# A planned attention-and-MLP kernel: two first groups of a stage interleaved, one product moved ahead in the last block, the engine order planned from longer durations

## The chip, the cores and the metric

The kernel runs on one core of one Trainium2 chip. The metric is the device time of one execution in microseconds (us), lower is better; of several runs the median counts.

## What is computed

The reference is a capped attention and two MLP blocks, each feeding the next (the weights arrive as 8-byte words, which the kernel itself turns into 4-byte floats):

```python
scores = scale * np.matmul(q, k.transpose(0, 1, 3, 2))     # 4 x 12 heads, 448 x 448, head size 64
scores = cap * np.tanh(scores / cap)
attn = np.exp(scores - max); attn = attn / (attn.sum(-1) + 1e-9)
x = (attn @ v) as 1792 tokens x 768
h = np.maximum(x @ w_in, 0.0);  x = h * h @ w_out          # 768 -> 2048 -> 768
gate = 1 / (1 + np.exp(-(x @ w_gate)));  val = x @ w_val   # 768 -> 1536
out = gate * val @ w_out2                                  # 1536 -> 768
```

## The kernel before, in words

The attention comes first and takes about the first 200 us. Then follow four **stages** (`STAGES`): two halves of 896 tokens of the first MLP (`x`, weights `w1`, `w2`), then two of the second (`y`, weights `wg`, `wv`, `wo`). Each half is worked on as a 2x2 split into blocks of 448 tokens, and the products use a Strassen scheme of seven products instead of eight. Every operand is split into a high part (fp32r, written by ACT) and a low part (written by DVE: raw minus high), so that a product of 128x128 by 128x448 is three matmuls (lines 742, 744, 745: low weight by high data, high weight by low data, high by high).

A **step** (a `unit` in the code) is one entry of TensorE's list; there are 550. `strassen` steps (nine matmuls) are named by a digit: "1" to "7", which stand for the data blocks b11 ("1"), b21 ("2"), b22 ("3") and the sums t2 ("6"), t4 ("4"), t3 ("7"), t1 ("5"). A group (two column blocks of one weight) has these seven, and within it they wait for each other: "1" and "2" meet in PSUM after an ACT copy of "1" (`pre`), "7" needs "6" copied out by ACT (`cp`), "4" needs "7" copied out, "3" needs "5" added up by DVE (`sum`). `second` steps are the products with `w2` (plain), `sums2` steps those with `wo` (again seven digits, six matmuls each, for three output columns c); a block of 21 `sums2` steps comes after each four columns (`add_block`), and works on data `gx` and `gy` that DVE and ACT make from the gated results `g`.

The list of steps is written by the loop at the end of the kernel (`add_s`, `add_q`, `add_p`, `add_block`): group after group as "12657", with "4" and "3" of the group before (`held`) behind "1" and "2" of the next. Behind TensorE, four engines run:

- DVE makes low parts, sums, the accumulations (`acc`) and four of the five operations that turn a weight into floats (lines 586, 588, 590, 592; `convert`); ACT does the first (line 230, `raw<-w`) once the attention is over, further high parts, copies out of PSUM and activations.
- POOL makes the low parts of the weights (line 733, `wl`).
- SP issues all transfers. A converted weight is written to DRAM (`s_w<-raw`) and read back (`pair<-s_w`) each time that it is used; the converter has two buffers `raw`, so the ACT operation of one weight waits for the store of the second one before it.

In which order each engine does its work isn't written by hand. A planner (`Flow`) plays the program through with a duration for each operation (`act`, `dve`, `dve1`, `dvep`, and a number at each `on(...)`) and writes each instruction down when it comes up in that play. The engines run their lists in that order, so a duration that is too short puts an instruction too early into its engine's list, and what stands behind it waits. When a weight is converted is bound to steps: `FIRST` and `AHEAD` in `convert_all` (weights of the second MLP: begin `FIRST` steps ahead of the first use, and spread from there). `early_forms` makes and stores the data blocks of the last stage as soon as its inputs are stored.

Of the kernel before, what the change touches and what calls it, by code (L numbers as in the profile page):

```python
# [14 lines left out]
ALU = mybir.AluOpType  # L15
# [14 lines left out]
SR = 32  # L30

PT, XE, TH, NV, WB = 2, 6, 2, 2, 4
WSTART, PACE, AHEAD, FIRST = 2, 2, 70, 180
# [21 lines left out]
class Flow:  # L55
# [6 lines left out]
    def __init__(self, have):  # L62
# [4 lines left out]
        self.free = {e: True for e in self.queue}  # L67
        self.pipe = 0.0
# [36 lines left out]
    def serve(self, engine):  # L105
# [11 lines left out]

        self.at(self.now + length, end)
# [27 lines left out]
    def dve(self, n):  # L146
        return lambda: (0.15 + n * 0.00104) * (1.0 if self.free["POOL"] else 1.6)

    @staticmethod
    def dve1(n):  # L150
        return 0.16 + n * 0.0005
# [13 lines left out]
def attn_mlp_kernel(ctx: ExitStack, tc: tile.TileContext, qk, v, cap, w1, w2, wg, wv, wo, out):  # L165
# [339 lines left out]
    def early_forms(src):  # L505
        w = WIDE[src[1]]
        for i in range(HK):
# [223 lines left out]
    def low(m, h, hi, lo, src, res, item):  # L731
        n = cols(src)
        yield on("POOL", 0.15 + n * 0.0023, lambda: nc.gpsimd.tensor_tensor(out=lo, in0=src, in1=f32(hi), op=ALU.subtract))  # L733
        flow.fire(("w", m, h))
        used(res, item)
# [135 lines left out]
    def sums2(u, stage, gi, num, c):  # L871
# [4 lines left out]
        elif num == "5":  # L876
            st["bank", grp, "e"] = bank(w)
# [5 lines left out]
        products(terms, o, num in "15", False)  # L883
        return shares2(grp, num, o, w)

    def shares2(grp, num, o, w):
# [15 lines left out]
        if num in "243":  # L902
            give(o)
        if num in "67" or gi < F2 // FG - 1:
            return
# [84 lines left out]
    def add_q(stage, gi, num, c):  # L990
        item = stage, "wo", gi
        if (item, num) not in spot:
# [8 lines left out]
            "3": [("out", grp, "5")]}.get(num, [])  # L1001
        units.append({"us": us(WIDE[STAGES[stage][1]], 6), "ms": [m], "needs": needs, "last": (stage, gi, num), "frees": 2, "tag": "gy" if num in "35" else "gx",
            "fn": sums2, "bank": {"1": 2, "5": 1}.get(num, 0), "args": (stage, gi, num, c)})

    def add_block(stage, gi, held, next_):
        nonlocal pairing, ahead
        order2 = [(num, c) for num in "1267453" for c in range(HK)]
        for x, (num, c) in enumerate(order2):
# [7 lines left out]
            add_q(stage, gi, num, c)  # L1016
# [18 lines left out]
    for stage, (src, _) in enumerate(STAGES):  # L1035
        kinds, kind2, ng = (("w1",), "w2", F1 // FG) if src == "x" else (("wg", "wv"), "wo", F2 // FG)
        w = WIDE[STAGES[stage][1]]
        held, wait = None, None
        for gi in range(ng):
            for j in range(2):  # L1040
                for kind in kinds:
                    grp = stage, kind, gi, j
                    for num in "12657":
                        if num != "1" or grp != ahead:
                            add_s(*grp, num)
                        if held and num in "12":
                            add_s(*held, "43"[num == "2"])
                    held = grp
                    if kind == "wg" and j == 0 and gi:
# [182 lines left out]
```

## Time and profile before

| | |
|---|---|
| time, median of 3 runs | 1165.56 us (1164.96 to 1168.18) |
| the profiled execution's own time | 1167.6 us |
| its span | 1165.8 us, mean granted TensorE clock 0.988 |
| busy: PE / PEld / DVE | 1104.3 (95%) / 924.8 (79%) / 878.9 (75%) us |
| busy: ACT / POOL | 683.1 (59%) / 491.4 (42%) us |

The page is read in this way: the busy shares tell which engine is nearest to the limit, but a busy TensorE is a modelled one; how densely its matmuls follow each other is told by counting them in a stretch. The waits tell for which engine TensorE stood still.

### The profile page before, as it was taken

Reading aid. Unit: us, or ns where it says so; the run is one execution under the profiler, and the core shown is the slowest. Engines: PE = TensorE matmul, PEld = TensorE weight load, DVE = VectorE, ACT = ScalarE, POOL = GpSimd, SP = SyncE. Lnnn points to the kernel's source line nnn. Section 1 sums busy time; section 2 is a strip of 40 time slices with the busy share of each in tenths; the row PEclk is TensorE's granted clock in tenths of the full one; section 3 lists DMA queues with packets and bytes.
Section 4 is the critical chain, followed back from the end, with each engine's and each line's share of the span. In section 5 each row is a group of like instructions: output and inputs, shape, how many; then the busy total and the mean of one; then the engine's idle time right before and its main releaser. Section 6 shows DMA issues by size and latency. Waiting matters only on the chain.

```text
span 1165.8 us, 16327 instructions
## 1 busy us (share of the span) xinstructions
PE 1104.3 (95%) x5700; PEld 924.8 (79%) x5700; DVE 878.9 (75%) x1171; ACT 683.1 (59%) x1152; POOL 491.4 (42%) x363
## 2 busy tenths in 40 slices
PE   7999999899999898999999989989999999999997
PEld 3444444798989797898999979888998899999996
DVE  3677788988988899778785999989767446257476
ACT  6878898556463666665546565645445355555351
POOL 0001000445453535344436266656555355655551
PEclk9999999999999999999999999999999899999999
DMA  4768876597877776968684354473236832241312
GB/s 134 234 203 280 278 245 213 186 294 232 260 239 245 231 290 210 319 238 294 209 288 145 140 186 153 149 266 141 70 134 233 318 116 92 84 133 57 103 65 95
DMA packets 83842, 227.44 MB, mean 195 GB/s; under 512 B 11824, under 2 KB 29744, under 8 KB 83760
## 3 DMA queue, kind: packets, MB, share of 16 engines
q1 hardware_dynamic: 83760, 226.40, 58.2%
q8 instruction: 45, 0.74, 0.3%
q14 instruction: 37, 0.30, 0.1%
HBM read 160.24 MB, written 65.95 MB: 194 GB/s over the span
## 4 chain that ended last, share of the span: by engine, by line
PE 60%; DVE 21%; DMA 11%; issue 4%; ACT 2%; SPq 2%; POOL 0%; DVEq 0%; ACTq 0%
PE pb L742 18%; PE pb L744 18%; PE pb L745 18%; DMA s_w<-raw 3%; PE pv L363 2%; DVE gx L233 2%; DVE raw L592 2%; DVE raw L590 2%; DMA sg<-xe 2%; DVE g L233 2%; DVE sums L233 1%; DVE raw L588 1%; DVE raw L586 1%; PE pv L378 1%; DMA z_w<-sums 1%
## 5 line engine op out<-in xcount | busy, mean ns | idle before, releaser
L733 POOL TENSOR_TENSOR wl<-pair,wh 128x384 fp32r<-128x384 f32 (+1 forms) x182 | 270.7, 1498 | 365.4 <-ACT wh L230 335.7
L733 POOL TENSOR_TENSOR wl<-sums,wh 128x384 fp32r<-128x384 f32 (+1 forms) x172 | 222.1, 1304 | 293.1 <-ACT wh L230 291.1
L744 PE MATMUL pb<-gx,wh 128*128 128x448 f32 x564 | 209.0, 371 | 9.7 <-DVE gx L233 9.7
L742 PE MATMUL pb<-gx,wl 128*128 128x448 f32 x564 | 207.5, 368 | 6.1 <-ACT gx L230 6.1
L745 PE MATMUL pb<-gx,wh 128*128 128x448 f32 x564 | 208.0, 369 | 0.0
L742 PE MATMUL pb<-t,wl 128*128 128x448 f32 x480 | 177.3, 369 | 9.8 <-ACT cp L230 8.5
L744 PE MATMUL pb<-t,wh 128*128 128x448 f32 x480 | 177.0, 369 | 0.5 <-DVE t L233 0.5
L745 PE MATMUL pb<-t,wh 128*128 128x448 f32 x480 | 176.4, 368 | 0.0
L230 ACT ACTIVATE wh<-pair 128x384 fp32r<-128x384 f32 (+1 forms) x182 | 111.0, 626 | 81.1 <-PE pb L745 68.7
L230 ACT ACTIVATE wh<-sums 128x384 fp32r<-128x384 f32 (+1 forms) x172 | 90.7, 541 | 95.5 <-PE pb L745 60.8
L742 PE MATMUL pb<-b,wl 128*128 128x448 f32 x360 | 133.2, 370 | 8.1 <-ACT pb L230 3.6
L744 PE MATMUL pb<-b,wh 128*128 128x448 f32 x360 | 132.6, 368 | 3.4 <-DVE b L233 3.4
L745 PE MATMUL pb<-b,wh 128*128 128x448 f32 x360 | 131.9, 366 | 0.0
L233 DVE TENSOR_TENSOR gx<-g,gx 128x448 fp32r<-128x448 f32 x124 | 107.0, 873 | 26.9 <-ACT gx L230 26.7
L744 PEld LDWEIGHTS pb<-gx,wh 128*128 128x128 f32 x564 | 107.1, 190 | 20.9 <-DVE gx L233 11.9
L742 PEld LDWEIGHTS pb<-gx,wl 128*128 128x128 f32 x564 | 108.0, 191 | 15.7 <-ACT gx L230 6.8
L745 PEld LDWEIGHTS pb<-gx,wh 128*128 128x128 f32 x564 | 107.5, 191 | 8.1
L742 PEld LDWEIGHTS pb<-t,wl 128*128 128x128 f32 x480 | 90.9, 189 | 21.0 <-issue 6.4
L744 PEld LDWEIGHTS pb<-t,wh 128*128 128x128 f32 x480 | 90.8, 189 | 8.3 <-DVE t L233 0.7
L745 PEld LDWEIGHTS pb<-t,wh 128*128 128x128 f32 x480 | 91.0, 190 | 7.6
L900 DVE TENSOR_TENSOR acc<-pb,acc 128x448 f32<-128x448 f32 x84 | 51.5, 621 | 52.6 <-PE pb L745 51.9
L592 DVE SCALAR_TENSOR_TENSOR raw<-w,raw 128x768 uint32<-128x768 uint32 x68 | 89.2, 1312 | 1.0
(99 smaller groups left out, 1904.9 us busy)
## 6 DMA issues: line engine op xcount, KB each, us to landing
w<-in_w_dram SPq DMA_DIRECT2D x32, 768.0 KB
pair<-s_w SPq DMA_DIRECT2D x56, 384.0 KB
s_w<-raw SPq DMA_DIRECT2D x32, 384.0 KB
qk<-in_qk_dram SPq DMA_DIRECT2D x24, 480.0 KB
w<-in_wg_dram SPq DMA_DIRECT2D x12, 768.0 KB
w<-in_wv_dram SPq DMA_DIRECT2D x12, 768.0 KB
w<-in_wo_dram SPq DMA_DIRECT2D x12, 768.0 KB
pair<-s_wo SPq DMA_DIRECT2D x24, 384.0 KB
```

The source lines that it names most:

```text
L230: return on("ACT", flow.act(cols(out)) + extra, lambda: nc.scalar.activation(out=out, in_=in_, func=func, **kw), rank)
L233: return on("DVE", flow.dve(cols(out)), lambda: nc.vector.tensor_tensor(out=out, in0=a, in1=b, op=ALU.subtract), rank)
L363: nc.tensor.matmul(out=o[j * D:(j + 1) * D, 0, :S], lhsT=st["v", n][:, c, j], rhs=pt, start=step == 0, stop=step == 3)
L378: nc.tensor.matmul(out=o[r:r + SR, 1, :S], lhsT=head[:, j] if step == 3 else ones, rhs=pt, start=step < 2, stop=step >= 2)
L586: yield on("DVE", flow.dve1(n), lambda: nc.vector.tensor_scalar(out=raw, in0=raw, scalar1=LOW, scalar2=HIGH, op0=ALU.max, op1=ALU.min), 2)
L590: yield on("DVE", flow.dve(n), lambda: nc.vector.scalar_tensor_tensor(out=mu, in0=lo, scalar=29, in1=mu, op0=ALU.logical_shift_right, op1= ...
L592: yield on("DVE", flow.dve(n), lambda: nc.vector.scalar_tensor_tensor(out=mu, in0=hi, scalar=0xC0000000, in1=mu, op0=ALU.bitwise_and, op1= ...
L733: yield on("POOL", 0.15 + n * 0.0023, lambda: nc.gpsimd.tensor_tensor(out=lo, in0=src, in1=f32(hi), op=ALU.subtract))
L742: nc.tensor.matmul(out=o, lhsT=wl, rhs=hi, start=first, stop=not stop, skip_group_check=not stop)
L744: nc.tensor.matmul(out=o, lhsT=wh, rhs=lo, start=False, stop=not stop, skip_group_check=not stop)
L745: nc.tensor.matmul(out=o, lhsT=wh, rhs=hi, start=False, stop=not stop or done_, skip_group_check=not stop)
L900: yield on("DVE", flow.dvep(w), lambda: nc.vector.tensor_tensor(out=acc, in0=o, in1=acc, op=ALU.add), 0)
```

## The change

Line numbers of the changed kernel are 8 to 23 higher. It has these parts:

- `TWO = (0, 1, 2)`: in the first three stages the first two groups A and B are listed as A1 B1 A2 B2 A6 A5 A7 B6 A4 B5 A3 B7, and not one after the other. In the third stage A is the gate's and B the value's group.
- In the last block of each half of the second MLP (`tail`), the three "3" steps (the product of b22, which needs no sum of results) come behind "2" instead of last. They open the third PSUM bank; "5" adds to it, and DVE now adds that bank to both halves of the output behind "5" (lines 909 and 917), each stored as soon as it is there.
- The planner's durations are longer: DVE operations are counted at double (`dve`) or one and a half times (`dve1`) when POOL has work waiting, and up to that when POOL is in one; `dve1` had no such factor and `dve` 1.6. A `wl` on POOL is 0.37 + n x 0.0022 us and not 0.15 + n x 0.0023.
- Conversion of the second MLP's weights begins 130 steps ahead of their first use, not 180; `early_forms` begins at step 150 at the earliest.
- The last outputs of the second stage are listed column by column.

```diff
+EARLY = 150
+TWO = (0, 1, 2)
-WSTART, PACE, AHEAD, FIRST = 2, 2, 70, 180
+WSTART, PACE, AHEAD, FIRST = 2, 2, 70, 130
...
     def dve(self, n):
-        return lambda: (0.15 + n * 0.00104) * (1.0 if self.free["POOL"] else 1.6)
+        return lambda: self.shared(0.15 + n * 0.00104, 2.0)
...
-        return 0.16 + n * 0.0005
+        return lambda: self.shared(0.16 + n * 0.0005, 1.5)
+    def shared(self, length, slow):
+        if self.queue["POOL"]:
+            return length * slow
+        return min(length * slow, length + max(0.0, self.end["POOL"] - self.now) * (1 - 1 / slow))
...
     def early_forms(src):
+        yield "until", ("unit", EARLY)
...
-        yield on("POOL", 0.15 + n * 0.0023, ...
+        yield on("POOL", 0.37 + n * 0.0022, ...
...
-        elif num == "5":
+        elif num == "5" or tail and num == "3":
             st["bank", grp, "e"] = bank(w)
...
+        if tail and num == "5":
+            if last_:
+                flow.spawn(finish(stage, x, off, w, acc))
+            x, off = c, w
+            acc = st["acc", stage, x][:, off:off + w]
+            yield on("DVE", flow.dvep(w), lambda: nc.vector.tensor_tensor(out=acc, in0=o, in1=acc, op=ALU.add), 0)
...
-        order2 = [(num, c) for num in "1267453" for c in range(HK)]
+        order2 = [(num, c) for num in ("1236745" if tail else "1267453") for c in range(HK)]
...
+            if gi == 0 and stage in TWO:
+                two = dict(zip("AB", groups_))
+                for x, num in ("A1", "B1", "A2", "B2", "A6", "A5", "A7", "B6", "A4", "B5", "A3", "B7"):
+                    if num != "1" or two[x] != ahead:
+                        add_s(*two[x], num)
+                held = two["B"]
+                groups_ = groups_[2:]
...
-                rest.sort(key=lambda x: x[1])
+                rest = [(x, off) for c in range(1, HK) for x in (c, c + HK) for off in (0, w) if x not in HALF]
```

What it moves, at three places. First **TensorE at the start of the second stage**: the first matmul of each step (nine to a step; `b11`, `b21`, `t2`, `t1`, `t3`, `t4` are the data blocks and sums named above, `pb` the PSUM bank, `wl` the low weight). Before:

```order
L742 MATMUL pb4_4397<-b21_4125,wl_4245 128x448 [waits Activation_49,Pool_49]
...
L742 MATMUL pb0_4396<-t2_4197,wl_4281 128x448 [waits Pool_49]
...
L742 MATMUL pb2_4482<-t1_4176,wl_4281 128x448 [waits Pool_49]
...
L742 MATMUL pb0_4396<-t3_4040,wl_4382 128x448 [waits Activation_49,Pool_49]
...
L742 MATMUL pb3_4525<-b11_3937,wl_4382 128x448 [waits Pool_49]
...
L742 MATMUL pb0_4396<-t4_4224,wl_4435 128x448 [waits Activation_49,Pool_49]
```

and now:

```order
L751 MATMUL pb4_4372<-b11_3912,wl_4194 128x448 [waits Pool_49]
...
L751 MATMUL pb0_4328<-b21_4082,wl_4247 128x448 [waits Activation_49,Pool_49]
...
L751 MATMUL pb2_4373<-b21_4082,wl_4247 128x448 [waits Activation_49,Pool_49]
...
L751 MATMUL pb3_4327<-t2_4146,wl_4339 128x448 [waits Pool_49]
...
L751 MATMUL pb6_4456<-t1_4101,wl_4339 128x448 [waits Pool_49]
...
L751 MATMUL pb3_4327<-t3_4016,wl_4385 128x448 [waits Activation_49,Pool_49]
```

B1 and B2 now stand around A2, so that each of the blocks b21, t2, t1 and t3 is first read one or two steps later than before. Second **DVE near the end of the first stage** (fourth group of four columns; `raw` is a weight in conversion, `gx` the low part of a result that the next product reads). Before:

```order
L586 TENSOR_SCALAR raw_3972<-raw_3972 128x768 [waits DMAHW6_49,Activation_49]
L588 TENSOR_SCALAR raw_3972<-raw_3972 128x768 [waits DVE_49]
L590 SCALAR_TENSOR_TENSOR raw_3972<-w64_3900,raw_3972 128x768 [waits DMAHW5_49,DVE_49]
L592 SCALAR_TENSOR_TENSOR raw_3972<-w64_3900,raw_3972 128x768 [waits DVE_49]
L233 TENSOR_TENSOR gx_4030<-g_3974,gx_4030 128x448 [waits Activation_49]
L239 TENSOR_TENSOR r_4051<-cp_4042,pb3_4003 128x448 [waits Activation_49]
```

and now:

```order
L247 TENSOR_TENSOR r_3964<-cp_3859,pb7_3848 128x448 [waits PE_49]
L241 TENSOR_TENSOR gx_3950<-g_3932,gx_3950 128x448 [waits Activation_49]
L241 TENSOR_TENSOR gx_3967<-g_3952,gx_3967 128x448 [waits Activation_49]
L241 TENSOR_TENSOR gx_4003<-g_3991,gx_4003 128x448 [waits Activation_49]
L247 TENSOR_TENSOR r_4023<-cp_4018,pb2_3974 128x448 [waits PE_49,Activation_49]
```

No weight is converted there any more: by the lists, DVE converts nine weights between steps 75 and 125 before and four now, none of them between steps 100 and 125; five more come behind step 200. Third **DVE at the very end**, behind TensorE's last three steps (`acc` is an output, `pb` the bank that is added). Before:

```order
L900 TENSOR_TENSOR acc_9660<-pb7_10953,acc_9660 128x448 [waits DVE_49,PE_49]
L900 TENSOR_TENSOR acc_9577<-pb2_10935,acc_9577 128x448 [waits PE_49]
L900 TENSOR_TENSOR acc_9587<-pb1_10944,acc_9587 128x448 [waits PE_49]
L900 TENSOR_TENSOR acc_9596<-pb7_10953,acc_9596 128x448 [waits PE_49]
```

and now:

```order
L909 TENSOR_TENSOR acc_9645<-pb3_10965,acc_9645 128x448 [waits DVE_49,PE_49]
L917 TENSOR_TENSOR acc_9583<-pb3_10965,acc_9583 128x448
L909 TENSOR_TENSOR acc_9653<-pb0_10974,acc_9653 128x448 [waits DVE_49,PE_49]
L917 TENSOR_TENSOR acc_9593<-pb0_10974,acc_9593 128x448
L909 TENSOR_TENSOR acc_9666<-pb5_10984,acc_9666 128x448 [waits DVE_49,PE_49]
L917 TENSOR_TENSOR acc_9602<-pb5_10984,acc_9602 128x448
```

Each of the last three steps is now followed by two additions, where one was.

## Rows read from the trace of the kernel before

**Rows 1.** Stretches of the span: start:end, length, busy us by engine, granted clock, DMA.

```profile
core 0: us, PE busy (x) PEld busy (x) DVE busy (x) ACT busy (x) POOL busy (x), PEclk, DMA share, GB/s
205.00:310.00 105.00, 99.39 (x483) 90.05 (x484) 96.40 (x117) 61.85 (x116) 49.74 (x32) 1.00 0.74 242
...
385.00:436.00 51.00, 46.24 (x220) 42.04 (x219) 44.78 (x59) 30.84 (x58) 20.04 (x13) 0.97 0.82 283
436.00:485.00 49.00, 41.86 (x193) 36.66 (x192) 47.28 (x57) 31.38 (x62) 21.14 (x14) 0.97 0.73 241
485.00:667.00 182.00, 180.23 (x888) 166.18 (x887) 135.26 (x174) 106.35 (x203) 81.25 (x58) 1.00 0.67 231
667.00:720.00 53.00, 47.85 (x217) 42.42 (x216) 49.25 (x64) 30.01 (x60) 32.72 (x24) 0.94 0.49 164
720.00:890.00 170.00, 164.65 (x798) 150.22 (x797) 139.85 (x176) 89.74 (x170) 101.93 (x72) 0.99 0.48 163
890.00:912.00 22.00, 17.71 (x74) 15.56 (x73) 19.43 (x25) 8.90 (x14) 8.98 (x5) 0.84 0.70 263
912.00:1130.00 218.00, 218.00 (x1076) 201.64 (x1075) 112.64 (x150) 109.48 (x216) 122.61 (x101) 1.00 0.35 114
1130.00:1166.00 36.00, 27.79 (x128) 24.72 (x126) 23.76 (x31) 7.71 (x13) 9.55 (x5) 0.95 0.20 77
```

**Rows 2.** Timeline, end of the first stage: start, duration, engine, line, instruction, [idle <-releaser].

```profile
402.84 2.22 DVE L233 TENSOR_TENSOR gx<-g,gx 128x448 fp32r<-128x448 f32 x1
...
405.12 0.47 PE L744 MATMUL pb<-gx,wh 128*128 128x448 f32 x1 [3.42 <-DVE gx L233]
```

**Rows 3.** Groups by line and form: conversion of weights on DVE (busy us, mean ns).

```profile
L592 DVE SCALAR_TENSOR_TENSOR raw<-w,raw 128x768 uint32<-128x768 uint32 x68 | 89.2, 1312 | 1.0
L590 DVE SCALAR_TENSOR_TENSOR raw<-w,raw 128x768 uint32<-128x768 uint32 x68 | 87.0, 1279 | 1.6
...
L588 DVE TENSOR_SCALAR raw<-raw 128x768 uint32<-128x768 uint32 x68 | 48.1, 708 | 1.3
L586 DVE TENSOR_SCALAR raw<-raw 128x768 f32<-128x768 f32 x68 | 45.8, 673 | 37.8 <-ACT raw L230 37.2
```

**Rows 4.** Timeline of TensorE, start of the second stage.

```profile
445.14 0.47 PE L744 MATMUL pb<-b,wh 128*128 128x448 f32 x1 [1.54 <-DVE b L233]
...
464.55 0.44 PE L742 MATMUL pb<-t,wl 128*128 128x448 f32 x1 [1.93 <-ACT cp L230]
...
476.72 0.47 PE L744 MATMUL pb<-gx,wh 128*128 128x448 f32 x1 [2.36 <-DVE gx L233]
```

**Rows 5.** Timeline of TensorE, start of the first stage.

```profile
230.04 0.44 PE L742 MATMUL pb<-t,wl 128*128 128x448 f32 x1 [1.66 <-ACT cp L230]
```

**Rows 6.** Timeline, start of the third stage: SP's queue, ACT and TensorE.

```profile
683.20 0.43 SPq L249 DMA_DIRECT2D s_wo<-raw  x1
...
693.20 0.89 ACT L230 ACTIVATE raw<-w 128x768 f32<-128x768 f32 x1 [3.43 <-DMA s_wo<-raw]
...
696.40 0.71 PE L742 MATMUL pb<-t,wl 128*128 128x448 f32 x1 [3.30 <-ACT cp L230]
```

**Rows 7.** Timeline of TensorE, last block of the third stage.

```profile
904.89 0.74 PE L742 MATMUL pb<-gx,wl 128*128 128x448 f32 x1 [4.29 <-ACT gx L230]
```

**Rows 8.** Timeline, last block of the fourth stage: DVE, TensorE and POOL.

```profile
1132.88 0.61 DVE L233 TENSOR_TENSOR gx<-g,gx 128x448 fp32r<-128x448 f32 x1
...
1140.00 0.47 PE L742 MATMUL pb<-gx,wl 128*128 128x448 f32 x1 [1.81 <-ACT gx L230]
...
1140.75 1.80 POOL L733 TENSOR_TENSOR wl<-sums,wh 128x768 fp32r<-128x768 f32 x1 [2.97 <-ACT wh L230]
...
1140.86 2.18 DVE L233 TENSOR_TENSOR gx<-g,gx 128x448 fp32r<-128x448 f32 x1
...
1143.09 0.74 PE L744 MATMUL pb<-gx,wh 128*128 128x448 f32 x1 [2.63 <-DVE gx L233]
```

**Rows 9.** Timeline of DVE, the last instruction of the program on an engine.

```profile
1162.27 0.62 DVE L900 TENSOR_TENSOR acc<-pb,acc 128x448 f32<-128x448 f32 x1 [0.59 <-PE pb L745]
```

More of the change, by code (lines that the diff above doesn't have):

```diff
@@ L67, in __init__ @@
         self.free = {e: True for e in self.queue}
+        self.end = dict.fromkeys(self.queue, 0.0)
         self.pipe = 0.0
@@ L116, in end @@
             self.serve(engine)
+        self.end[engine] = self.now + length
         self.at(self.now + length, end)
@@ L901, in shares2, with finish @@
         flow.fire(("out", grp, num))
-        if num in "243":
+        last_ = gi == F2 // FG - 1
+        if tail and num == "5":
[4 more added lines that the diff above has]
+            yield on("DVE", flow.dvep(w), lambda: nc.vector.tensor_tensor(out=acc, in0=o, in1=acc, op=ALU.add), 0)
+        if num in ("2453" if tail else "243"):
             give(o)
-        if num in "67" or gi < F2 // FG - 1:
-            return
+        if last_ and num in ("245" if tail else "2453"):
+            yield from finish(stage, x, off, w, acc)
+    def finish(stage, x, off, w, acc):
         t0 = START[STAGES[stage][1]] + off
@@ L1037, in attn_mlp_kernel @@
         w = WIDE[STAGES[stage][1]]
-        held, wait = None, None
+        held = None
         for gi in range(ng):
[L1040 to L1049, printed above, removed]
-                        held = add_block(stage, gi - 1, held, (stage, "wv", gi, 0))
+            groups_ = [(stage, kind, gi, j) for j in range(2) for kind in kinds]
+            if gi == 0 and stage in TWO:
[5 more added lines that the diff above has]
+                groups_ = groups_[2:]
+            for grp in groups_:
+                for num in "12657":
+                    if num != "1" or grp != ahead:
+                        add_s(*grp, num)
+                    if held and num in "12":
+                        add_s(*held, "43"[num == "2"])
+                held = grp
+                if grp[1] == "wg" and grp[3] == 0 and gi:
+                    held = add_block(stage, gi - 1, held, (stage, "wv", gi, 0))
             if src == "y":
                 if gi == ng - 1:
-                    ahead = (stage + 1, "wg", 0, 0)
-                    held = add_block(stage, gi, held, ahead if stage == 2 else None)
+                    add_block(stage, gi, held, (stage + 1, "wg", 0, 0) if stage == 2 else None, True)
                 continue
```

23 lines of the change are left out of this document (11 added, 12 removed).

## The prediction

> **What bounds the kernel now.** I read the stretches of the span first, because TensorE's busy time tells little here: a matmul's end is modelled, so I count matmuls. Between 912 and 1130 us nothing holds TensorE up: 1076 matmuls in 218.00 us [rows 1], 0.2026 us each. By that spacing every other stretch has a loss, its length less its count times 0.2026:
>
> 205 to 310: 105 - 483 x 0.2026 = 7.1 us; 385 to 436: 51 - 44.6 = 6.4; 436 to 485: 49 - 39.1 = 9.9; 485 to 667: 182 - 179.9 = 2.1; 667 to 720: 53 - 44.0 = 9.0; 720 to 890: 170 - 161.7 = 8.3; 890 to 912: 22 - 15.0 = 7.0; 1130 to the last matmul (DVE's last addition begins behind it at 1162.27 [rows 9], so some 32.1 us): 32.1 - 128 x 0.2026 = 6.2 [rows 1].
>
> That is 56 us, and it is all that an edit of the order can win behind the attention; the matmuls stay the same in number. The kernel is bound by TensorE, with gaps in which it waits for DVE or ACT. So I went to the timelines of the gaps, and looked in each for what stood in the queue of the engine that was late. The reader is to see three kinds: a chain that is simply longer than the steps that cover it [rows 4, 5, 7, 8], weight conversion that stands in DVE's queue in front of a low part [rows 2], and an ACT operation that waits for a store, with a copy out of PSUM behind it [rows 6].
>
> **The change part by part.** The sum is made against the profiled execution's own 1167.6 us (span 1165.8 and 1.8 around it); that is 2.0 above the median of 1165.56.
>
> *Conversions leave the end of the first stage.* The wait of 3.42 us at 405.12 is for a low part that took DVE 2.22 us from 402.84, behind two weights in conversion [rows 2]. The four operations of a weight take 1312 + 1279 + 708 + 673 = 3972 ns on average [rows 3], and DVE was busy for 44.78 of the 51 us [rows 1]. By the lists there is no conversion now between steps 100 and 125, which is this stretch. The loss of 6.4 can shrink by that one wait, 3.4, or wholly; as both the wait and the half-speed clock behind it (0.97 granted on average) have the same source, I take 5.5.
>
> *Two groups interleaved, second stage.* Three waits of 1.54, 1.93 and 2.36 us make most of the loss of 9.9 [rows 4]: for the low part of b21, for a copy of "6" in front of "7", and for a low part of a result. Each step lasts 9 x 0.2026 = 1.8 us, and the new list puts one or two steps of the other group between each of these and its source. Apart from that `early_forms` now starts at step 150, so its work leaves a stretch in which DVE was busy for 47.28 of 49 us [rows 1]. Left over could be 8 us, if only the first wait goes, or nothing; I take a gain of 7, because all three waits are shorter than the two steps that now cover them.
>
> *Two groups interleaved, first stage.* The longest wait is 1.66 us for a copy in front of "4" [rows 5]; it keeps its one step of cover, so this gap may stay. The loss of 7.1 contains conversions that are as dense as before. I take 2, between 0 and 4. What was filled with the group's first step between the two halves of the last attention output is now filled with nothing; that costs little, since the same step only moves behind it.
>
> *Two groups interleaved, third stage.* The largest wait is another kind. A converted weight is stored at 683.20 [rows 6]; ACT wants the buffer and stands until 693.20, 3.43 us of it idle, and the copy that TensorE's "7" needs is behind it, so TensorE loses 3.30 us. No edit shortens a store. In the new list the same operation stands about two steps behind its store, 3.6 us, where this store took 10.0. So I take only 2.5 of the 9.0, for the waits of the first steps, between -3 and 6.
>
> *b22 ahead, last block, twice.* The chain from the group's last product over gate, differences and splits to "6" takes as long as before, but now three steps of six matmuls stand in it, 18 x 0.2026 = 3.6 us. Third stage: the wait is 4.29 and the matmuls behind it last 0.74 us against 0.47 behind shorter waits [rows 7, 4], granted clock 0.84 in the stretch [rows 1], so part ran at 1.2 and not 2.4 GHz. Cover 3.6, less one or two additions of 0.62 [rows 9] that DVE now has inside the chain, plus a little clock: 4 of 7.0, between 2 and 5.5. Fourth stage: waits of 1.81 and 2.63 [rows 8]; 3.2 of 6.2, between 1.5 and 5. At the very end one more addition stands in front of the last store: +0.6 [rows 9].
>
> *The work that was moved.* Five conversions, 5 x 4.0 = 20 us of DVE, go behind step 200, and `early_forms` behind 485 us. DVE is busy there for 135.26 of 182 us and 139.85 of 170 [rows 1], so there is room, but the two `raw` buffers are taken in quicker succession. Nothing at all, or two waits with the stretch of [rows 6] around them (about 6 us each): 0 to 12, I take 3, near the lower end because in 485 to 667 some fifteen conversions, by the list, already cost only 2.1.
>
> *Longer durations* cost nothing by themselves. What they give is in the terms above; for the remaining 8.3 of 720 to 890 I take nothing.
>
> Here one row speaks against the edit. The low part of a 128x448 result takes DVE 0.61 us alone and 2.18 when it starts at 1140.86, under POOL's 1.80 from 1140.75 [rows 8]; the planner's new price for it is at most (0.15 + 448 x 0.00104) x 2 = 1.2. So under a wide POOL operation DVE's work is still planned too short by 1.0 us.
>
> The Trainium skill (SBUF — State Buffer, "Who interferes with whom") says that a DVE instruction with two SBUF inputs and a GpSimd instruction that reads SBUF exclude each other, the later one standing still until the earlier has ended. By that rule no factor is right: it would be what is left of POOL's operation plus DVE's own. For this row it gives 1142.55 - 1140.86 + 0.61 = 2.3 us, and the 2.18 measured agrees. By the rule the forecast would be that of the first rival below.
>
> Sum: -5.5 - 7 - 2 - 2.5 - 4 - 3.2 + 0.6 + 3 = -20.6; 1167.6 - 20.6 = 1147. Against the median instead of the profiled execution it would be 1145; I forecast **1146 us**.
>
> **The rivals.**
>
> *The prices stay too short.* DVE operations under a wide POOL operation last 2.2 and not 1.2 us, so the new lists put work too early as well, and the chains of the last blocks, in which POOL prepares four wide weights, grow with it. Then the cover of "3" is eaten (4 + 3.2 becomes 3), and the second stage keeps half of its loss (7 becomes 3.5). Gain 20.6 - 4.2 - 3.5 - about 2 from the first stage = 11: 1156 to 1157 us. For it speaks [rows 8]; against it that most `wl` are half as wide, and that conversions are gone from the worst places by number of step and not by price.
>
> *A wait on the raw buffer takes the place, slower.* ACT's operation at the head of a conversion waits for a store, here 10.0 us after its issue [rows 6], and everything behind it on ACT with it, first the copies that TensorE needs. From step 200 on conversions come in pairs now. One such wait costs TensorE 3.3 us and about 6 of a stretch's 9.0 together with the lower clock. The gains without the last term are 23.6, so from four such waits there is nothing left, and with five it is 1167.6 - 23.6 + 30 = 1174. Against it: in 485 to 667, with some fifteen conversions, all waits together cost 2.1 [rows 1].
>
> *The waits only move.* All four queues have a new order, and each gap that closes hands TensorE earlier to the next late engine: 1163 to 1168, no change.
>
> *More than I grant.* If the third stage's wait goes too, the middle stretch loses 4 less and the moved work costs nothing: -20.6 - 4 - 4 - 3 = -31.6, 1136 us.
>
> **How the numbers follow.** Forecast 0.62 (1139 to 1153), prices too short 0.15, more than granted 0.10, only moved 0.07, slower 0.06. The range reaches over the first two and half of the third: 1136 to 1160. What can be told from no change is 0.3%, 3.5 us: faster 0.62 + 0.15 + 0.10 = 0.87, the same 0.07, slower 0.06.
>
> **What would show it.** In the new profile the stretch in front of the second stage should hold some 247 matmuls in 51 us, and the 49 us behind it about 227. "6" of the last blocks should wait under 3 us, and the end should be two additions 0.6 us apart. A third-stage start with ACT still at `raw<-w` for over 3 us is expected. I am wrong if TensorE waits over 3 us between steps 200 and 370 several times (the moved work), if the second stage still waits for low parts (the prices), or if the attention in front, which I count as unchanged though its DVE order differs, is longer than about 205 us.

## The result and the profile after

The changed kernel takes **1151.78 us** (median of 4 runs, 1150.06 to 1152.91) against 1165.26 us for the kernel before (4 runs): ratio 0.9858, 95% interval 0.9829 to 0.9887. It is faster by 13.5 us, which is 1.2% by the two medians (0.9884) and 1.4% by the ratio on record. The profiled executions differ by 14.7 us (1152.91 and 1167.6; spans 1151.1 and 1165.8). A later series (e10) gave 1153.74 against 1167.29, ratio 0.9887 (0.9862 to 0.9912). The forecast was 1146 with a range from 1136 to 1160: the direction was right, the gain was six us smaller than forecast.

The stretches of the new span, cut where the stages now stand, answer to [rows 1]:

```profile
core 0: us, PE busy (x) PEld busy (x) DVE busy (x) ACT busy (x) POOL busy (x), PEclk, DMA share, GB/s
208.50:310.00 101.50, 96.84 (x462) 88.29 (x459) 89.45 (x109) 63.67 (x118) 48.70 (x28) 0.97 0.75 247
...
386.00:437.00 51.00, 50.44 (x250) 46.40 (x249) 30.72 (x48) 32.81 (x64) 20.75 (x17) 1.00 0.58 192
437.00:486.00 49.00, 48.91 (x241) 44.71 (x240) 39.56 (x48) 34.19 (x65) 26.02 (x18) 1.00 0.74 251
486.00:657.00 171.00, 170.94 (x842) 157.54 (x841) 150.99 (x186) 106.49 (x199) 79.87 (x54) 1.00 0.76 267
657.00:710.00 53.00, 47.71 (x222) 42.20 (x221) 49.66 (x70) 30.22 (x61) 26.92 (x21) 0.97 0.38 142
710.00:880.00 170.00, 162.27 (x790) 147.14 (x789) 165.07 (x187) 91.22 (x173) 110.86 (x75) 1.00 0.54 190
880.00:905.00 25.00, 21.77 (x100) 19.15 (x99) 22.58 (x29) 9.67 (x16) 13.13 (x8) 0.95 0.70 263
...
1118.00:1151.00 33.00, 26.76 (x130) 23.80 (x128) 26.14 (x35) 8.01 (x13) 10.27 (x5) 1.00 0.22 84
```

With the prediction's measure (length less matmuls times 0.2026; the last stretch up to 1146.86, where DVE's last pair of additions begins) each term of the sum can be set beside what it became:

| term | loss before | loss after | forecast | measured |
|---|---|---|---|---|
| attention (first MLP step at 208.59; before, second step at 204.88, less the 1.84 of the first, which stood inside the attention) | | | 0 | +5.5 |
| first stage, start | 7.1 | 7.9 | -2 | +0.8 |
| first stage, end | 6.4 | 0.4 | -5.5 | -6.0 |
| second stage, start | 9.9 | 0.2 | -7 | -9.7 |
| 485 to 667 and 720 to 890 (moved work) | 2.1 + 8.3 | 0.4 + 9.9 | +3 | 0 |
| third stage, start | 9.0 | 8.0 | -2.5 | -1.0 |
| third stage, last block | 7.0 | 4.7 | -4 | -2.3 |
| fourth stage, last block | 6.2 | 2.5 | -3.2 | -3.7 |
| one addition more at the end (two, 0.54 apart) | | | +0.6 | +0.5 |
| sum | | | -20.6 | -15.9 |

The profiled executions differ by 14.7; the rest is rounding at the edges of stretches. The stretch from 310 to 385 us, which the prediction's list leaves out, lost 2.3 us before (359 matmuls in 75 us) and loses 2.2 now (364 in 76, from 310 to 386), so nothing is missing there. Behind the attention the sum of the forecast was nearly right in this profile, -20.6 against -21.4. What is missing stands in front of it. This is TensorE there, the second output from last, the last one and the first MLP step:

```profile
192.15 4.92 PE L371 MATMUL pv<-pt,v 128*64 128x448 f32 x16 [2.69 <-DVE xe L250]
...
202.10 4.92 PE L371 MATMUL pv<-pt,v 128*64 128x448 f32 x16 [2.58 <-ACT pt L238]
...
208.59 0.47 PE L751 MATMUL pb<-b,wl 128*128 128x448 f32 x1
```

and DVE's queue between the two copies that empty the PSUM tile which the last output needs:

```profile
198.78 0.62 DVE L250 COPY xe<-pv 128x448 f32<-128x448 f32 x1 [2.28 <-PE pv L386]
199.32 0.61 DVE L241 TENSOR_TENSOR t<-tm,t 128x448 fp32r<-128x448 f32 x1
199.97 0.62 DVE L241 TENSOR_TENSOR tm<-b,tm 128x448 f32<-128x448 f32 x1
200.52 0.62 DVE L426 TENSOR_TENSOR xe<-xe,th 128x448 f32<-128x448 f32 x1
201.05 0.26 DVE L414 SCALAR_TENSOR_TENSOR sg<-sg,eps 16x56 f32<-16x56 f32 x1
201.24 0.60 DVE L250 COPY xe<-pv 128x448 f32<-128x448 f32 x1
```

The same place in the kernel before:

```profile
191.55 3.23 PE L363 MATMUL pv<-pt,v 128*64 128x448 f32 x16 [0.51 <-DVE xe L242]
...
196.49 1.16 DVE L242 COPY xe<-pv 128x448 f32<-128x448 f32 x2 [0.77 <-PE pv L378]
...
197.90 1.72 PE L363 MATMUL pv<-pt,v 128*64 128x448 f32 x8 [0.67 <-ACT pt L230]
...
198.26 1.40 ACT L230 ACTIVATE pt<-pt,capa 128x1344 f32<-128x1344 f32 x1
...
204.88 0.47 PE L742 MATMUL pb<-b,wl 128*128 128x448 f32 x1
```

Before, both copies stood back to back (196.49 to 197.65) and TensorE went on at 197.90 after 0.67 us idle; now four other operations stand between them and it waits 2.58, 1.9 us longer. The view names ACT's exponential, which now ends at 201.96, 0.12 behind the copy. But before, the first half of the output started while that exponential had not begun (198.26), so the half doesn't read it; the copy is what it lacks.

That is one part of the 5.5 us. The second output from last waits too, for a copy that stood on DVE behind an operation that waited for a load (`th`):

```profile
190.76 0.62 DVE L426 TENSOR_TENSOR xe<-xe,th 128x448 f32<-128x448 f32 x1 [0.82 <-DMA th<-rd]
...
191.49 0.60 DVE L250 COPY xe<-pv 128x448 f32<-128x448 f32 x1
```

TensorE had come there 1.6 us sooner than before, so with 2.69 us of waiting instead of 0.51 it starts 0.6 us later. The 16 matmuls of each of the two outputs then take 4.92 us instead of 3.23. The granted clock is 0.66 from 192 to 197 us, 1.00 from 197 to 202 and 0.66 from 202 to 207, so a part of them ran at 1.2 and not at 2.4 GHz; that makes 1.7 and 1.3 us. Together: 0.6 + 1.7 + 1.9 + 1.3 = 5.5.

In the first stage's start the wait for the copy in front of "4" [rows 5] is gone. Two others stand there instead, one for the low part of a result and one for a low weight:

```profile
233.55 0.74 PE L753 MATMUL pb<-gx,wh 128*128 128x448 f32 x1 [1.98 <-DVE gx L241]
...
242.88 0.47 PE L751 MATMUL pb<-gx,wl 128*128 128x448 f32 x1 [2.23 <-POOL wl L742]
```

In the third stage's start the wait behind a store [rows 6] is gone, against what I expected; others make nearly the same loss:

```profile
669.48 0.47 PE L751 MATMUL pb<-t,wl 128*128 128x448 f32 x1 [1.18 <-POOL wl L742]
...
676.95 0.47 PE L751 MATMUL pb<-t,wl 128*128 128x448 f32 x1 [1.09 <-POOL wl L742]
...
690.10 0.44 PE L751 MATMUL pb<-t,wl 128*128 128x448 f32 x1 [1.90 <-ACT cp L238]
```

The copy in front of 690.10 stood on ACT behind an operation that waited for DVE's `r`, and that stood behind a conversion and, from 686.23 to 687.60, a difference of weights:

```profile
688.16 0.58 ACT L238 ACTIVATE r<-r 128x448 f32<-128x448 f32 x1 [2.98 <-DVE r L247]
...
684.55 1.76 DVE L601 SCALAR_TENSOR_TENSOR raw<-w,raw 128x768 uint32<-128x768 uint32 x1
```

In the last blocks "6" no longer waits in the third stage (4.29 before [rows 7]); "7" does, for an addition (`acc`) that stood on DVE behind the gate's differences and low parts, one of them 2.25 us long beside a POOL operation:

```profile
900.22 0.44 PE L751 MATMUL pb<-gx,wl 128*128 128x448 f32 x1 [2.41 <-DVE acc L909]
...
894.57 2.25 DVE L241 TENSOR_TENSOR g<-g 128x448 f32<-128x448 f32 x1
...
1131.24 0.47 PE L753 MATMUL pb<-gx,wh 128*128 128x448 f32 x1 [0.80 <-DVE gx L241]
1135.61 0.44 PE L751 MATMUL pb<-gx,wl 128*128 128x448 f32 x1 [1.26 <-DVE acc L909]
```

### The profile page after: what moved, and what is told of

Its sections match the earlier page's. It is cut to its first block, busy times and chain, and to the rows that moved or that the text cites. A ratio compares the mean times of both kernels' runs of the same rounds, so it can differ in the third digit from the quotient of the medians.

```text
span 1151.1 us, 16343 instructions
## 1 busy us (share of the span) xinstructions
PE 1102.6 (96%) x5700; PEld 922.2 (80%) x5700; DVE 897.8 (78%) x1176; ACT 685.6 (60%) x1153; POOL 496.4 (43%) x363
## 4 chain that ended last, share of the span: by engine, by line
PE 48%; DVE 17%; issue 3%; ACT 2%; DMA 2%; POOL 1%; SPq 0%; DVEq 0%; ACTq 0%
PE pb L751 16%; PE pb L753 16%; PE pb L754 16%; DVE gx L241 2%; DVE g L241 2%; DVE sums L241 2%; DVE raw L601 2%; DVE g L801 1%; DVE raw L599 1%; DMA s_wv<-raw 1%; DVE acc L909 1%; DVE raw L597 1%; DVE raw L595 1%; DVE r L247 1%; DVE acc L241 1%
## 5 line engine op out<-in xcount | busy, mean ns | idle before, releaser
L742 POOL TENSOR_TENSOR wl<-pair,wh 128x384 fp32r<-128x384 f32 (+1 forms) x182 | 275.3, 1525 | 394.5 <-ACT wh L238 388.1
L751 PE MATMUL pb<-gx,wl 128*128 128x448 f32 x564 | 207.0, 367 | 10.4 <-DVE acc L909 4.4
L241 DVE TENSOR_TENSOR gx<-g,gx 128x448 fp32r<-128x448 f32 x124 | 124.3, 1012 | 23.2 <-ACT gx L238 23.0
L751 PEld LDWEIGHTS pb<-t,wl 128*128 128x128 f32 x480 | 90.8, 189 | 15.9 <-POOL wl L742 6.6
L247 DVE TENSOR_TENSOR r<-cp,pb 128x448 f32<-128x448 f32 x80 | 49.1, 614 | 56.2 <-ACT cp L238 38.1
L371 PE MATMUL pv<-pt,v 128*64 128x448 f32 x384 | 80.9, 565 | 11.0 <-DVE xe L250 8.5
```

The source lines that it names most:

```text
L241: return on("DVE", flow.dve(cols(out)), lambda: nc.vector.tensor_tensor(out=out, in0=a, in1=b, op=ALU.subtract), rank)
L247: return on("DVE", flow.dvep(cols(out)), lambda: nc.vector.tensor_tensor(out=out, in0=sb, in1=bank, op=op), rank)
L371: nc.tensor.matmul(out=o[j * D:(j + 1) * D, 0, :S], lhsT=st["v", n][:, c, j], rhs=pt, start=step == 0, stop=step == 3)
L742: yield on("POOL", 0.37 + n * 0.0022, lambda: nc.gpsimd.tensor_tensor(out=lo, in0=src, in1=f32(hi), op=ALU.subtract))
L751: nc.tensor.matmul(out=o, lhsT=wl, rhs=hi, start=first, stop=not stop, skip_group_check=not stop)
```

## The experiments

For all profiles I added up what TensorE loses by groups of steps: for each MLP matmul the time since the start of the one before, less 0.2042 us (what the planner counts for one). "MLP from" is the start of the first MLP step, or where that stands between the halves of the last output, the start of the second less 1.84. Steps 402 to 528 lose nothing in any of them (-0.9 to -1.2 by this measure) and are left out. The ratio is to the kernel before in the same series (medians there 1166.3 to 1167.5 from e1 on).

| kernel | median us | ratio (95%) | MLP from | 0-29 | 30-126 | 127-254 | 255-284 | 285-380 | 381-401 | 529-549 |
|---|---|---|---|---|---|---|---|---|---|---|
| before | 1165.26 | 1 | 203.0 | 3.7 | 11.6 | 11.0 | 9.0 | 7.5 | 7.2 | 6.2 |
| changed | 1151.78 | 0.9858 (0.9829-0.9887) | 208.6 | 7.6 | 2.9 | -0.4 | 7.9 | 9.2 | 5.4 | 2.4 |
| e10 changed again | 1153.74 | 0.9887 (0.9862-0.9912) | 207.4 | 7.6 | 3.2 | 0.4 | 6.2 | 16.2 | 3.9 | 2.4 |
| e1 first plain | 1148.03 | 0.9827 (0.9798-0.9855) | 203.9 | 6.0 | 1.2 | -0.5 | 7.9 | 16.1 | 3.8 | 2.4 |
| e2 step between | 1150.86 | 0.9864 (0.9824-0.9904) | 206.1 | 4.7 | 5.7 | -0.6 | 6.3 | 15.4 | 4.5 | 2.4 |
| e3 b22 last | 1157.69 | 0.9921 (0.9891-0.9951) | 206.3 | 7.6 | 3.3 | -0.6 | 7.9 | 9.8 | 6.3 | 6.8 |
| e4 conversions, forms early | 1152.23 | 0.9878 (0.9851-0.9904) | 205.9 | 3.9 | 10.6 | 6.7 | 3.7 | 8.1 | 5.4 | 2.4 |
| e5 second plain | 1154.72 | 0.9869 (0.9841-0.9897) | 206.3 | 3.9 | 6.2 | 3.3 | 4.6 | 14.9 | 4.2 | 2.4 |
| e6 old durations | 1173.67 | 1.0043 (1.0023-1.0063) | 205.1 | 8.0 | 9.9 | 8.5 | 8.4 | 11.2 | 4.1 | 4.8 |
| e7 exclusive durations | 1183.42 | 1.0120 (1.0094-1.0145) | 200.5 | 4.4 | 2.0 | 2.9 | 11.8 | 41.7 | 10.5 | 1.3 |
| e8 conversions early | 1152.50 | 0.9854 (0.9826-0.9882) | 205.2 | 3.4 | 7.4 | 7.3 | 3.8 | 10.0 | 4.7 | 2.4 |
| e9 only durations | 1159.86 | 0.9939 (0.9916-0.9962) | 202.4 | 6.6 | 1.3 | 17.4 | 7.1 | 7.5 | 7.4 | 5.9 |
| e11 attention exclusive | 1151.74 | 0.9877 (0.9851-0.9903) | 201.6 | 4.3 | 7.8 | 0.8 | 6.3 | 9.3 | 6.5 | 2.4 |
| e12 idle POOL | 1148.20 | 0.9825 (0.9797-0.9854) | 201.2 | 6.5 | 2.9 | 0.0 | 5.7 | 10.4 | 11.7 | 2.4 |

The groups of each row are those of one execution, the medians those of all. The executions of one kernel in a series lie 2 to 11 us apart from the fastest to the slowest (the kernel before up to 14), so a group can differ by some us from one execution to the next, as 285-380 does for the changed kernel.

**The attention.** e1:

```diff
-TWO = (0, 1, 2)
+TWO = (1, 2)
```

> The changed kernel with the first stage's two groups one after the other again (the other two starts stay interleaved). In the changed kernel the attention ends about 5.5 us later than before (first MLP step at 208.59 against an equivalent of 203.04), and steps 0 to 29 lose 7.6 us against 3.7. Theory A, the interleaving of the first stage did both (other order of weights and loads, first step no longer between the halves of the last attention output): the attention ends at about 203 again and the first 30 steps lose about 3.7, so 1152.9 - 5.5 - 3.9 = 1143.5 us. Theory B, the longer durations reordered DVE in the attention: the last attention output still waits over 2 us and the kernel gains at most the 3.9 of the first steps, 1149 us or more.

1148.03 us, and the MLP begins at 203.9: both copies stand together again.

```profile
197.19 1.16 DVE L250 COPY xe<-pv 128x448 f32<-128x448 f32 x2 [1.37 <-PE pv L386]
```

```profile
198.75 1.72 PE L371 MATMUL pv<-pt,v 128*64 128x448 f32 x8 [0.83 <-ACT pt L238]
```

So theory A, the interleaving of the first stage, holds for the attention. The second half of that theory, on steps 0 to 29, doesn't hold: their loss went from 7.6 to 6.0 only, and in e4, e5 and e8 this group loses under 4 with the stage interleaved: that loss isn't the interleaving's.

e2 puts the first step back between the halves:

```diff
-            if kind == "V" and done(("t", n, s), ("v", n)) and (s or have("pvb")):
+            hold = n == last and s == 2 and not pe["u"]
+            if kind == "V" and not hold and done(("t", n, s), ("v", n)) and (s or have("pvb")):
```

> The changed kernel, but the plan holds the second half of the last attention output back until the first MLP step has been listed, so that this step stands between the halves as it did before. If the lost cover is what costs: the wait for exp (2.58 us in front of the last output) becomes work of 1.84 us, 1.7 to 1.9 us gained, and up to 1.7 more if the output's matmuls run at the full clock again: 1149.5 to 1151.2 us. If the order on DVE and SP in front of it is the cause and not the missing step: the wait moves to the step, no change, 1152.5 to 1153.5.

1150.86 us, not told apart from the changed kernel, and the MLP begins at 206.1. The wait in front of the last output stayed (2.68 us): the order in front of it costs, not the step that is gone.

e10 is the changed kernel itself:

> The changed kernel once more, for its attention. In its first profile the first MLP step started at 208.59; in e3, e4 and e8, which write the same instructions up to there, at 206.3, 205.9 and 205.2. If the 5.5 us by which the attention was longer belong to its order: 208 to 209 again. If half of it is chance: 205 to 206.5. The time 1150 to 1153 either way.

207.4. The six profiles with the first stage interleaved, the changed kernel's durations and no step between the halves begin the MLP at 205.2 to 208.6, mean 206.6; e1, e9 and e12, with it plain (one group after the other), at 201.2 to 203.9, mean 202.5. e6, interleaved with the old durations, has 205.1. So about 4 us belong to the order and up to 2 of the first profile's 5.5 to chance.

One part of the 4 is the same everywhere: the wait in front of the last output is 2.58 to 2.68 us in the six and in e2, and 0.67 to 0.83 before and in e1, e9 and e12. The rest changes. In e10 the granted clock stays at 1.00 there and both outputs take 3.23 us, but its second output from last already starts 2.8 us later than before. What makes this rest is not shown.

**b22's product.** e3:

```diff
-                    add_block(stage, gi, held, (stage + 1, "wg", 0, 0) if stage == 2 else None, True)
+                    add_block(stage, gi, held, (stage + 1, "wg", 0, 0) if stage == 2 else None)
```

> The changed kernel with b22's product last again in the last blocks. In the changed kernel these two blocks lose 5.4 and 2.4 us, before 7.2 and 6.2, and the end has one addition more (0.6). If b22's place did this: 1152.9 + 1.8 + 3.8 - 0.6 = 1157.9 us. If the longer durations did it: no more than 1 us, 1152 to 1154.

1157.69, and the two waits for the high part of "6" are back (4.29 before, and 1.81 and 2.63). The median is 4.0 to 5.9 us above the changed kernel's two, so this part of the change is worth somewhat less than the 6.6 that its terms say together.

```profile
893.61 0.74 PE L751 MATMUL pb<-gx,wl 128*128 128x448 f32 x1 [4.42 <-ACT gx L238]
...
1129.22 0.74 PE L751 MATMUL pb<-gx,wl 128*128 128x448 f32 x1 [3.35 <-ACT gx L238]
```

**Conversions and interleaving.** e4 and e8:

```diff
-EARLY = 150
+EARLY = 0
...
-WSTART, PACE, AHEAD, FIRST = 2, 2, 70, 130
+WSTART, PACE, AHEAD, FIRST = 2, 2, 70, 180
```

> The changed kernel with conversion beginning 180 steps ahead again and the last stage's data blocks made as early as they can be. If the conversions' place made the gains at the end of the first stage and in its middle: steps 30 to 105 lose 6.6 and not 2.4, steps 106 to 126 lose 5.0 and not 0.5, and the start of the second stage stays near 0.2 because the interleaving covers it: 1152.9 + 8.7 = 1161.6 us. If the longer durations made these gains: less than 2 us more, 1153 to 1155. If the second stage's gain came from its emptier DVE and not from the interleaving, its first 30 steps lose 3 us or more again.

e8 has the second of these lines alone:

> The changed kernel with conversion beginning 180 steps ahead again, the early data blocks from step 150 as changed. In e4, with both put back, steps 30 to 156 lost 17.7 us against 3.1. If the conversions made that: over 10 us are lost there here too, about 1154 with what the third stage gives back (3.7 lost at its start in e4, 7.9 in the changed kernel). If the early data blocks made it: under 6.

Steps 30 to 254 lose 17.3 and 14.7 us instead of 2.6, though the second stage is interleaved, and e8 shows that it is the conversions and not the early forms. But the third stage loses less (17.2 and 18.5; 22.5 and 26.2 in the two profiles of the changed kernel), and in the medians nothing is left: 1152.2 and 1152.5. Beginning the conversions later moved a loss from the first half to the third stage. e5 has the second stage plain (`TWO = (0, 2)`):

> The changed kernel with the second stage's two groups one after the other again (first and third interleaved). The first 30 steps of that stage lost 9.8 us before and 0.2 in the changed kernel; with the conversions and the early data blocks put back (e4) they lost 7.1 although interleaved. If the interleaving is needed as well: 4 us or more are lost there again, 1156 us or more. If the emptier DVE alone did it: under 2 us there, 1152 to 1154.

2.9 us are lost in its first 30 steps instead of 0.2, and the time, 1154.72, can't be told from e10's.

**The durations.** e6 is the changed kernel planned with the old ones:

```diff
-        return lambda: self.shared(0.15 + n * 0.00104, 2.0)
+        return lambda: (0.15 + n * 0.00104) * (1.0 if self.free["POOL"] else 1.6)
...
-        return lambda: self.shared(0.16 + n * 0.0005, 1.5)
+        return 0.16 + n * 0.0005
...
-        yield on("POOL", 0.37 + n * 0.0022, ...
+        yield on("POOL", 0.15 + n * 0.0023, ...
```

> The changed kernel, planned with the durations of the kernel before (DVE factor 1.6 or none, the low weight on POOL 0.15 + n x 0.0023); list of steps, conversions and early data blocks as changed. If the longer durations carry a part of the gain: the groups of steps 30 to 105, 255 to 400 or the last blocks lose 4 us or more beyond the changed kernel's, 1156 us or more. If what they give is little, as my sum had it: 1150 to 1154.

1173.67 us: not only is the whole gain gone, the new lists alone are slower than the kernel before (ratio 1.0043, 1.0023 to 1.0063). Its profiled execution (1169.65) was the fastest of twelve. In it the first two stages lose 16 us more than in the changed kernel (steps 30 to 254); the second stage's start shows one place. TensorE waits 4.09 us for a low part that stands on DVE behind a conversion, and both run beside POOL:

```profile
471.37 0.47 PE L753 MATMUL pb<-gx,wh 128*128 128x448 f32 x1 [4.09 <-DVE gx L241]
```

```profile
466.71 2.45 DVE L599 SCALAR_TENSOR_TENSOR raw<-w,raw 128x768 uint32<-128x768 uint32 x1
469.09 0.61 DVE L247 TENSOR_TENSOR r<-cp,pb 128x448 f32<-128x448 f32 x1
469.62 1.70 DVE L241 TENSOR_TENSOR gx<-g,gx 128x448 fp32r<-128x448 f32 x1
```

```profile
466.37 4.47 POOL L742 TENSOR_TENSOR wl<-pair,wh 128x768 fp32r<-128x768 f32 x2 [2.33 <-ACT wh L238]
```

e9 is the other corner: the kernel before, with e6's lines the other way round and nothing else of the change.

> The kernel before, planned with the changed kernel's longer durations and nothing else of the change (lists of steps, conversions, early data blocks and the last blocks as before). In e6 the changed kernel without them lost all of its gain. If the durations carry most of the gain by themselves: TensorE loses under 45 us behind the attention (before 54.9, changed kernel 33.9), 1153 to 1158 us. If they are only needed so that the new lists can win: over 50, 1163 to 1168.

1159.86 us, between the two expectations. The durations alone gain 7.4 us by the medians. The profiled execution was the slowest of eleven (1164.02); in it steps 30 to 126 lose 1.3 instead of 11.6, but the second stage loses 6.4 more than before, where the next row shows the low part of b21 late. Together with the new lists they gain 13.5: the parts don't add up (-7.4 and +6.2).

```profile
438.03 0.74 PE L750 MATMUL pb<-b,wh 128*128 128x448 f32 x1 [3.32 <-DVE b L239]
```

**Other durations.** e7 (on e1):

```diff
     def dve(self, n):
-        return lambda: self.shared(0.15 + n * 0.00104, 2.0)
+        return lambda: self.shared(0.15 + n * 0.00104)
...
-    def shared(self, length, slow):
...
+    def shared(self, length):
+        self.lock = max(self.now, self.end["POOL"]) + length
+        return self.lock - self.now
+
+    def pool(self, n):
+        return lambda: max(self.now, self.lock) - self.now + 0.15 + n * 0.0022
...
-        yield on("POOL", 0.37 + n * 0.0022, ...
+        yield on("POOL", flow.pool(n), ...
```

> The kernel of e1 with other durations in the plan: a DVE operation on SBUF alone begins when POOL's operation has ended and then takes its own length, and POOL's likewise behind DVE's; no factors. In e1 the third stage loses 7.9 + 16.1 + 3.8 = 27.8 us, 7.7 of it at one step for a low weight that took POOL 8.29 us while DVE worked without a gap. If the factors, which make DVE's operations at most twice as long, put the work in the wrong order: the third stage loses under 20 us and the time is about 1140. If who wins between DVE and POOL is settled by the moment and not by the order: the third stage still loses 24 or more, 1145 to 1151.

1183.42, the slowest. By its list seven conversions stand as late as steps 360 to 380, and TensorE loses about 52 us in the third stage's second part. The longest wait there is for a low weight that these conversions made late:

```profile
905.54 0.74 PE L755 MATMUL pb<-gx,wl 128*128 128x448 f32 x1 [14.52 <-POOL wl L746]
```

Durations made after the rule that fits the row at 1140.86 [rows 8] made a worse plan, by where the conversions fell in it.

e11 uses them until the attention ends:

> The kernel of e1, with the durations of e7 (a DVE operation behind POOL's, no factors) while the attention runs and the changed kernel's longer ones afterwards. e7 had the attention over at 200.5 (its second step at 202.38, less one step of 1.84) against 203.9 in e1 and 203.0 before, and lost in the third stage what the plan put late there. If the attention's order made the first: 3 us less than e1, about 1145. If it was chance: 1147 to 1149.

1151.74, no gain over e1. The MLP begins at 201.6, but its second step then loses 3.2 us (1.1 in e1): TensorE came sooner to operands that were not ready sooner.

**POOL shut out.** In e1, e2, e5 and e10 step 297 loses 6.6 to 6.7 us, in the first profile of the changed kernel and in e3 nothing, with the same instructions up to there as in e10. That first profile, DVE and POOL:

```profile
743.77 5.14 DVE L599 SCALAR_TENSOR_TENSOR raw<-w,raw 128x768 uint32<-128x768 uint32 x2
748.83 5.12 DVE L601 SCALAR_TENSOR_TENSOR raw<-w,raw 128x768 uint32<-128x768 uint32 x2
```

```profile
739.30 2.12 POOL L742 TENSOR_TENSOR wl<-sums,wh 128x768 fp32r<-128x768 f32 x1 [9.25 <-ACT wh L238]
743.51 4.59 POOL L742 TENSOR_TENSOR wl<-pair,wh 128x768 fp32r<-128x768 f32 x2 [2.08 <-ACT wh L238]
```

and e10, the same kernel, POOL, DVE and TensorE:

```profile
737.22 8.23 POOL L742 TENSOR_TENSOR wl<-sums,wh 128x768 fp32r<-128x768 f32 x1 [9.08 <-ACT wh L238]
...
740.24 1.81 DVE L599 SCALAR_TENSOR_TENSOR raw<-w,raw 128x768 uint32<-128x768 uint32 x2
741.98 1.81 DVE L601 SCALAR_TENSOR_TENSOR raw<-w,raw 128x768 uint32<-128x768 uint32 x2
...
745.51 0.74 PE L751 MATMUL pb<-gx,wl 128*128 128x448 f32 x1 [5.47 <-POOL wl L742]
```

In the first, POOL's low weight (`wl<-sums`) takes 2.1 us, and DVE's four operations, beside POOL's next ones, 10.3; in the other the same low weight takes 8.2 and DVE's four 3.6. e12 takes two conversions away from behind that low weight:

```diff
+        while "mlp" in flow.done and not flow.free["POOL"]:
+            yield "for", 0.2
         yield on("DVE", flow.dve1(n), lambda: nc.vector.tensor_scalar(
             out=raw, in0=raw, scalar1=LOW, scalar2=HIGH, op0=ALU.max, op1=ALU.min), 2)
```

> The kernel of e1, but after the attention the plan lets DVE begin a weight's conversion only while POOL has nothing to do. In e1, e2, e5 and e10 step 297 lost 6.6 to 6.7 us: a low weight that took POOL 8.29 us in e1, begun under a row of DVE operations without a gap, nine of them behind it in DVE's list, four of these two weights in conversion at once. Here five stand behind it. If DVE's unbroken work keeps POOL's operation from going on: that operation takes under 6 us, step 297 loses under 3, and the time is 4 us under e1's, about 1144, if no weight comes late. If POOL's operation was late for another reason (the store or the load of its sums): step 297 loses over 5 as before, 1147 to 1150. If weights come late by it: TensorE waits at steps 300 to 400 for pairs, and 1150 or more.

```profile
727.54 5.78 POOL L744 TENSOR_TENSOR wl<-sums,wh 128x768 fp32r<-128x768 f32 x1 [8.59 <-ACT wh L238]
```

```profile
730.72 0.94 DVE L603 SCALAR_TENSOR_TENSOR raw<-w,raw 128x768 uint32<-128x768 uint32 x1
```

POOL's operation ends 1.66 us behind DVE's last one (731.66 and 733.32), as in e10 (743.79 and 745.45), and TensorE's step with it: it now loses 4.2 instead of 6.6, not under 3. In e1, e2 and e5 it ends 1.66 us behind as well. With five DVE operations behind it instead of nine the operation takes 5.78 us instead of 8.2 to 8.3, so DVE's row is what kept it. The time, 1148.20, is e1's; one reason is that another low weight came late. The difference of weights it is made from stands last on DVE behind the gate's work (at 886.06), and b22's product, now early in the block, waits for it:

```profile
889.83 0.74 PE L753 MATMUL pb<-gy,wl 128*128 128x448 f32 x1 [9.06 <-POOL wl L744]
```

e1 and e12, both with the first stage plain, have the best medians, 1148.0 and 1148.2: 18 to 19 us under the kernel before. Against the changed kernel that is 4 to 6 us; the intervals of e1 and e10 do not overlap, those of e1 and the first series do.

## Why the prediction was right, and where it was not

*What bounds the kernel* held: behind the attention TensorE's loss fell from 54.9 to 33.9 us, 21.0, and the forecast's sum for that part was 20.6. That the two agree so well is in part luck: in e10's profile of the same kernel the loss is 38.6, a fall of 16, and among the terms the second stage and the moved work came out 5.7 us better than forecast, the first stage's start, the third stage's start and its last block 6 us worse.

*The attention in front* is the step that failed. The prediction says of the order there "which I count as unchanged though its DVE order differs", and so gave it no term. It cost 5.5 us in the first profile and 4.4 in e10; the sign named for it, longer than about 205 us, came with 208.6. That the step between the halves "costs little" holds (e2): what costs is the order on DVE. The part that every interleaved profile shows is the last output's wait for the second copy out of PSUM, which the plan now put behind four DVE operations, 1.9 us. The rest of the first profile's 5.5 is above all the slower matmuls, 3.0, which e10 doesn't have.

*Conversions leave the end of the first stage*: -6.0 for -5.5, but the cause is not the one named alone. With the conversions put back (e8, e4) and with the durations alone (e9) steps 106 to 126 lose nothing either (-0.3, -0.3 and 0.5; 5.0 before), and nothing with the conversions moved and the old durations (e6, 0.3): there one of the two is enough. e9 has the whole gain of steps 30 to 126 without moving a conversion, e6 hardly any of it (9.9 lost). The low part that was late before [rows 2] stood behind the conversions and also beside POOL:

```profile
402.27 2.31 POOL L733 TENSOR_TENSOR wl<-pair,wh 128x768 fp32r<-128x768 f32 x1 [1.75 <-ACT wh L230]
```

*Two groups interleaved, second stage*: -9.7 for -7. I argued that two steps of cover do it. They don't by themselves: interleaved, steps 127 to 254 lose 8.5 with the old durations (e6) and 7.3 with the conversions early (e8); plain they lose 17.4 with the durations alone (e9) and 3.3 with everything else (e5). By these profiles all three are needed.

*Two groups interleaved, first stage*: +0.8 for -2, and the 4 us of the attention; by e1 and e12 the one part that is better undone. The copy's wait that I expected to stay went, and waits of 1.98 and 2.23 us for a low part and a low weight came. *Third stage*: -1.0 for -2.5. The store wait that I expected to stay went; two waits for low weights (1.18 and 1.09) and one for a copy behind DVE's work (1.90) took its place. Whether the second stage's last outputs, now listed column by column, have a part in this was not run.

*b22 ahead*: -2.3 and -3.7 for -4 and -3.2, plus 0.5 for the addition; e3 gives the sum back, 5.3 by the groups. The rest of the third stage's wait went to the additions in front of "7".

*The work that was moved*: 0 for +3 in the first profile, but in e10 steps 285 to 380 lose 16.2 us (7.5 before), 6.6 of them at step 297, and not by the buffer `raw` as I had it: by conversions that keep POOL out.

*Longer durations* "cost nothing by themselves. What they give is in the terms above": as a whole they do cost nothing (e9 gains 7.4 us), though with them alone the second stage loses 6.4 more. But as a part of the change they were valued at nothing, and e6 lacks 20 us without them.

*The rivals.* "The prices stay too short" was named for a real mechanism: DVE's operations beside a wide POOL operation still last 2.25 us, and 2.5 in conversions. The Trainium skill (SBUF — State Buffer, "Who interferes with whom") has a DVE instruction with two SBUF inputs and a GpSimd instruction that reads SBUF exclude each other, and says that the order of issue decides which of them stands still. That one of the two stands still is what the rows show: DVE's conversions in one profile (10.3 us), POOL's low weight in the other (8.2). What decides which, they don't show: in e10 POOL's was begun in front of nine DVE operations and stood behind all of them. The plan that goes by this rule (e7) was the slowest, so prices taken from it did not win here; whether prices that are still too short limit the gain stays open. "A wait on the raw buffer" came only small: ACT stands at most 2.50 us for a store in the first profile (at 737.57), and between steps 200 and 370 TensorE loses over 3 us at no step there and at one, 297, in e10; "the waits only move" holds for one part, the conversions' start.

## What to carry to other kernels

Where a planner sets the order, an edit of the list changes the order everywhere, also in a part that it doesn't touch: compare all queues there, and look first at copies that free a PSUM tile. Value a change of the planner's durations by itself and together with the rest: here the lists alone lose 6 us, the durations alone win 7, and together they win 13.5. And do not take one profile's wait as the order's: the same instructions lost 0 or 6.6 us at one step.

## What I had not expected of the hardware

A POOL operation that was begun under DVE's unbroken work did not get its turn between two DVE operations: it stood through nine of them in e1, e2, e5 and e10, 8.2 to 8.3 us for one of 1.8, and through five in e12, 5.8 us, and in all five profiles it ended 1.66 us behind the last. In the other profile, where POOL had two operations in a row, each of the four DVE operations beside them took some 2.6 us instead of 0.9. Which of the two happens changed between executions of one kernel; what decides it I have not found out.
